# Two weight clamps moved to ScalarE, with conversions, outputs and differences issued at other places

## The chip, the cores and the metric

One core of a Trainium2 chip runs the whole program. Five engines take part: TensorE (PE, with its weight loads PEld), VectorE (DVE), ScalarE (ACT), GpSimd (POOL) and SyncE (SP, which here issues loads and stores). Each engine runs its own list of instructions in order and waits for others by semaphores. The metric is the time of one execution on the device in microseconds (us), as the median of several runs.

## The reference, cut to what matters

```python
# attention: batch 2, seq 3008, d_model 256, d_qk 64
scores = matmul(z, z.transpose(0, 2, 1)) / S
x = u * matmul(maximum(scores, 0.0) ** 2, v)        # 6016 tokens of 256
# first network: w_in 256 x 2048, w_out 2048 x 256
h = x @ w_in;  x = (h - tanh(h)) @ w_out
# second network, with weights of its own
h = x @ w_in
g = where(h >= 1, h, where(h <= -1, 0, (h + 1) ** 2 / 4))
x = g @ w_out
```

The weights come as 64-bit floating point words; the kernel turns them into 32-bit ones itself.

## The kernel before

**Attention.** For each batch, six chunks `c` of 512 queries (the last 448) go over 12 pairs `t` of key tiles, 144 pairs in all, counted here from 0. An *own* pair has its scores `sc` made by TensorE (L361); ScalarE takes the Relu `r` (L386) and the square `hi` (L389), the square at full precision (`a` or `ax`) is made by ScalarE (L397) or in chunk 0 also by VectorE (L404), and VectorE makes the remainder `lo` (L409). The product with `v` (L424) takes `hi` and `lo` one after the other, 16 and 8 matmuls. A *mirrored* pair (those in `MIRROR`) makes no scores: the block was made and stored by an earlier chunk (`mir<-ax`), comes back as `m`, is transposed in two steps by VectorE (`am`, L329), rounded by ScalarE (L343), and VectorE makes `lo` (L347). The product of a pair runs two pairs behind its scores (`LAG`).

**A chunk's end.** Of four accumulators ScalarE copies two to `y` (L469), VectorE adds the other two (L470), and then multiplies by `u` in `scaled` (`ut<-y`, L478). `scaled` is put on the list `deferred`, which `flush` empties in a step of the next chunk.

**Weights.** There are 32 pieces (16 units of weights, each with an input and an output half). For each, the generator `convert` issues seven steps on VectorE and yields a price after each: two masks (L207, L209), two clamps of the exponent `e` (L213, L217), the two parts of the mantissa put together (L215), the sign (L219), the product (L224, to `win` or `wout`). Three later steps stand on the list `posts`: sums on GpSimd, the rounding `phin` or `phout` on ScalarE (L240), the remainder `plin` or `plout` on VectorE (L245). `work(amount)` adds its amount to a credit and issues steps while it is positive. In attention `make(i)` calls it with `CONVERT[0]` for an own pair of chunks 1 to 5 other than a chunk's first; in the first network `fill` calls it with `CONVERT[1]`.

**Networks.** Both run in units of 512 tokens by 128 hidden columns, as seven products of differences and sums of blocks. TensorE puts a product into a bank `m` (L656), ScalarE and VectorE take it out (L592, L595), apply the function (L608, L618), round it (L592) and make its remainder (L629), and TensorE multiplies by the output weights (L675). The differences of the first unit (`t`, L531) and their parts `xht` (ScalarE, L550) and `xlt` (VectorE, L566) are made beside the last pairs of attention; the list `mid` holds those of its steps that run within the unit itself, and the last pair's `lo` among them.

**What sets the order.** All engines' orders follow from the order in which this program issues; no scheduler moves anything later.

## Time and profile before

| what | value |
|---|---|
| median of 3 runs | 1446.07 us (1445.56 to 1447.16) |
| the profiled execution, on the device | 1448.0 us |
| its span from first to last instruction | 1446.2 us |
| TensorE busy | 1426.9 us, 99% |
| VectorE busy | 1250.8 us, 86% |
| ScalarE busy | 983.5 us, 68% |
| GpSimd busy | 106.2 us, 7% |
| mean granted TensorE clock | 0.998 |

TensorE is the busiest engine. What it lacks are single stretches in which it waits. They are found in the list of waits and looked at one by one in the engines' order of time. In a row of that view the first number is the start in us from the span's start, the second the time of the row's instructions together, and in brackets stands how long the engine was idle before and what released it. Instructions of an engine overlap: the next one often starts 0.06 to 0.1 us before the one ahead is shown as ended.

### The profile page before, as it was taken

The page shows a single profiled execution, that of the slowest core. Times are in us where ns is not written, and L with a number is a line of the kernel's source. Part 1 is how long each engine was busy: PE and PEld are TensorE (multiplying, and loading weights), DVE is VectorE, ACT ScalarE, POOL GpSimd, SP SyncE. Part 2 cuts the span into 40 slices and gives each one's busy share as a digit, 9 for nine tenths or more (in the row PEclk, how much of TensorE's full clock was granted, in tenths as well). Part 3 has the DMA queues.
Part 4 walks back from the last instruction along what each step waited for, and adds up shares of the span by engine and source line. Part 5 has one row for each costly group of instructions (what it writes and reads, how often), then busy time and mean ns, then how long its engine had stood idle before and what let it go on. Part 6 is the DMA issues. An engine that isn't in the chain of part 4 may idle for free.

```text
span 1446.2 us, 22024 instructions
## 1 busy us (share of the span) xinstructions
PE 1426.9 (99%) x8293; PEld 1187.9 (82%) x8293; DVE 1250.8 (86%) x1551; ACT 983.5 (68%) x1209; POOL 106.2 (7%) x163
## 2 busy tenths in 40 slices
PE   9999999999999999999999999999999999999998
PEld 6888788988777888888888888987888878788897
DVE  7989899898988888898988888889888888988775
ACT  8887657888654767767676767666666666666543
POOL 0122010031100011010101010000000000000000
PEclk9999999999999999999999999999999999999999
DMA  8899996799898557383765747482564644456361
GB/s 197 256 309 258 245 215 153 233 294 273 240 238 263 182 177 296 114 311 122 259 242 188 273 168 299 137 305 93 170 223 174 204 166 134 161 182 226 119 204 26
DMA packets 274203, 301.11 MB, mean 208 GB/s; under 512 B 134960, under 2 KB 210608, under 8 KB 274096
## 3 DMA queue, kind: packets, MB, share of 16 engines
q1 hardware_dynamic: 261408, 258.53, 57.4%
q0 software_dynamic: 11488, 40.90, 8.0%
q8 instruction: 65, 1.06, 0.3%
q10 hardware_dynamic: 1200, 0.26, 0.1%
q14 instruction: 42, 0.34, 0.1%
HBM read 225.84 MB, written 73.79 MB: 207 GB/s over the span
## 4 chain that ended last, share of the span: by engine, by line
PE 78%; DVE 9%; ACT 5%; DMA 3%; SPq 3%; issue 2%; DVEq 0%; ACTq 0%
PE acc L675 31%; PE m L656 27%; PE acc L424 13%; PE h L849 3%; PE sc L361 2%; DVE lo L409 2%; PE acc L885 2%; DMA m<-mir 1%; DVE am L329 1%; PE acc L906 1%; SPq L316 1%; DVE lo L347 1%; ACT r L386 1%; ACT gha L592 1%; DMA mir<-ax 1%
## 5 line engine op out<-in xcount | busy, mean ns | idle before, releaser
L424 PE MATMUL acc<-hi,v 64*128 64x512 f32 (+1 forms) x2256 | 289.3, 384 | 2.3 <-DVE y L470 2.2
L424 PEld LDWEIGHTS acc<-hi,v 64*128 64x128 f32 x2256 | 225.6, 184 | 39.9 <-DVE y L470 4.7
L656 PE MATMUL m<-xht,w 128*128 128x512 f32 (+1 forms) x704 | 216.1, 388 | 0.0
L675 PE MATMUL acc<-ghb,w 128*128 128x512 f32 (+1 forms) x704 | 187.8, 388 | 0.0
L675 PE MATMUL acc<-gha,w 128*128 128x512 f32 (+1 forms) x704 | 173.3, 387 | 0.0
L424 PE MATMUL acc<-lo,v 64*128 64x512 f32 (+1 forms) x1104 | 158.0, 387 | 7.4 <-DVE lo L409 4.4
L675 PEld LDWEIGHTS acc<-ghb,w 128*128 128x128 f32 x704 | 131.1, 188 | 28.1 <-ACT ghb L592 0.3
L675 PEld LDWEIGHTS acc<-gha,w 128*128 128x128 f32 x704 | 132.2, 188 | 26.3
L656 PEld LDWEIGHTS m<-xht,w 128*128 128x128 f32 x704 | 132.5, 188 | 25.5
L618 DVE TENSOR_TENSOR ta<-ha,ta 128x1024 f32<-128x1024 f32 (+1 forms) x88 | 107.0, 1216 | 40.4 <-ACT ta L615 29.4
L656 PE MATMUL m<-xlt,w 128*128 128x512 f32 (+1 forms) x352 | 137.8, 392 | 2.5 <-DVE xlt L566 1.2
L629 DVE TENSOR_TENSOR gla<-ta,gha 128x1024 fp32r<-128x1024 f32 (+1 forms) x88 | 106.7, 1213 | 33.8 <-ACT gha L592 32.9
L424 PEld LDWEIGHTS acc<-lo,v 64*128 64x128 f32 x1104 | 110.5, 184 | 30.4 <-DVE lo L409 9.7
L592 ACT ACTIVATE u<-m 128x512 f32<-128x512 f32 (+1 forms) x176 | 102.6, 583 | 35.3 <-PE m L656 34.0
L592 ACT ACTIVATE ghb<-tb 128x1024 fp32r<-128x1024 f32 (+1 forms) x88 | 92.6, 1053 | 47.8 <-DVE tb L618 46.9
L629 DVE TENSOR_TENSOR glb<-tb,ghb 128x1024 fp32r<-128x1024 f32 (+1 forms) x88 | 106.5, 1210 | 16.9 <-ACT ghb L592 16.3
L618 DVE TENSOR_TENSOR tb<-hb,tb 128x1024 f32<-128x1024 f32 (+1 forms) x88 | 106.5, 1210 | 5.0 <-ACT tb L608 0.2
L343 ACT ACTIVATE hi<-am 128x1024 fp32r<-128x1024 f32 (+1 forms) x60 | 61.4, 1023 | 70.0 <-DVE am L329 56.5
L656 PE MATMUL m<-xhb,w 128*128 128x512 f32 (+1 forms) x352 | 107.7, 387 | 0.0
L592 ACT ACTIVATE gha<-ta 128x1024 fp32r<-128x1024 f32 (+1 forms) x88 | 92.2, 1048 | 17.8 <-DVE ta L618 17.1
L386 ACT ACTIVATE r<-sc 128x1024 f32<-128x1024 f32 (+1 forms) x83 | 84.1, 1013 | 27.7 <-PE sc L361 26.1
L615 ACT ACTIVATE ta<-ta 128x1024 f32<-128x1024 f32 x40 | 42.4, 1061 | 78.4 <-DVE ta L610 78.4
(115 smaller groups left out, 2538.0 us busy)
## 6 DMA issues: line engine op xcount, KB each, us to landing
w<-packed SPq DMA_DIRECT2D x288, 512.0 KB, 6.4
mir<-ax SPq DMA_DIRECT2D x50, 512.0 KB, 4.5
m<-mir SPq DMA_DIRECT2D x200, 128.0 KB, 4.5
xr<-kept SPq DMA_DIRECT2D x20, 512.0 KB, 7.2
packed<-phin POOLq DMA_DIRECT2D x16, 512.0 KB, 4.1
packed<-plin POOLq DMA_DIRECT2D x16, 512.0 KB, 4.7
widein<-in_moe_w_in_dram POOLq DMA_DIRECT2D x15, 512.0 KB, 6.7
wideout<-in_moe_w_out_dram POOLq DMA_DIRECT2D x15, 512.0 KB, 8.1
```

Of the source, the lines that this page charges most:

```text
L343: nc.scalar.activation(out=hi[s], in_=a[s], func=AF.Copy)
L361: nc.tensor.matmul(ps[:, j, :n], zs[b, g][half, x, k0 : k0 + P], q[half, y, :n], start=(k == 0), stop=(k == 2))
L386: nc.scalar.activation(out=r[s], in_=ps[s], func=AF.Relu)
L409: lows.append(lambda: nc.vector.tensor_tensor(out=lo_, in0=to, in1=hi_, op=ALU.subtract))
L424: nc.tensor.matmul(acc[d][h][:, :n], lhsT, g[half, j, :n], start=start, stop=stop)
L592: nc.scalar.activation(out=out_, in_=in_, func=AF.Copy)
L615: nc.scalar.activation(out=self.t[self.s], in_=self.t[self.s], func=AF.Square, scale=0.5, bias=0.5)
L618: nc.vector.tensor_tensor(out=self.t[self.s], in0=self.h[self.s], in1=self.t[self.s], op=ALU.subtract if self.net == 0 else ALU.max,)
L629: nc.vector.tensor_tensor(out=self.lo[self.s], in0=self.t[self.s], in1=self.hi.bitcast(F32)[self.s], op=ALU.subtract)
L656: nc.tensor.matmul(bank[:, : self.w], self.win[wp][:, block, :], xop[self.net, self.s][x][xp], start=start and i == 0, stop=True, skip_gro ...
L675: nc.tensor.matmul(self.acc(d, n)[:, : self.w], self.wout[:, part, j, d * P : (d + 1) * P], g[:, at, : self.w], start=start, stop=stop,)
L849: nc.tensor.matmul(banks[j][:, :n], win[wp][:, 2 * k + j, :], x[:, k, :n], start=(k == 0 and i == 0), stop=(k == 1 and i == 2),)
```

## The change

It has five parts.

1. In `convert`, the two clamps of the exponent are two Relu of ScalarE where `state["scalar"]` is set: in chunks 2 to 5 and in the first network. 52 instructions of VectorE go and 52 of ScalarE come; 12 clamps stay on VectorE, in chunk 1. The price of both is then not counted in the credit. The product's yields and the moment at which the next piece's load is issued move along.
2. `make` issues no conversion in a chunk's first three pairs; `CONVERT[0]` is 2.0 instead of 1.8, the credit is cut at 2.0, and no new steps start while three or more wait in `posts`. A mirrored pair issues a step from `posts` that costs nothing by the prices (the sums on GpSimd or the rounding on ScalarE). At the end of attention 16 pieces are done instead of 18; the first network converts the rest.
3. `scaled` is issued by the new list `scales`, behind the second score product of the next chunk; in chunks 2 to 5 that is behind the two transposes of a mirrored pair.
4. In a chunk's second pair the full-precision square by VectorE (`product`, chunk 0) is put on the list `tail`, and so comes behind the adds of `y`.
5. In the first unit of the first network, the first four steps of `mid` (two differences, their rounding, the last pair's `lo`) come ahead of the add of `ha`; one `z` block at the start is transposed and cut a pair later.

TensorE's order stays as it was. On GpSimd and SyncE a few loads change places.

```diff
-CONVERT = 1.8, 1.4
+CONVERT = 2.0, 1.4
...
-        return [(dma, AHEAD), (turn, 3), (cut, 2)]
+        late = (b, g) == (0, 2)
+        return [(dma, AHEAD), (turn, 3 - late), (cut, 2 - late)]
...
-        nc.vector.tensor_scalar(out=es, in0=ei, scalar1=-896.0 * 2**20, scalar2=0.0, op0=ALU.add, op1=ALU.max)
-        yield 0.42
+        if state["scalar"]:
+            nc.scalar.activation(out=e, in_=es, func=AF.Relu, scale=-8.0, bias=1151.0 * 2**23)
+            nc.scalar.activation(out=es, in_=e, func=AF.Relu, scale=-1.0, bias=255.0 * 2**23)
+        else:
+            nc.vector.tensor_scalar(out=es, in0=ei, scalar1=-896.0 * 2**20, scalar2=0.0, op0=ALU.add, op1=ALU.max)
+            nc.vector.tensor_scalar(out=es, in0=es, scalar1=255.0 * 2**20, scalar2=8.0, op0=ALU.min, op1=ALU.mult)
+            yield 0.84
         nc.vector.scalar_tensor_tensor(out=m, in0=low, scalar=2.0**-32, in1=mi, op0=ALU.mult, op1=ALU.add)
         yield 0.69
-        nc.vector.tensor_scalar(out=es, in0=es, scalar1=255.0 * 2**20, scalar2=8.0, op0=ALU.min, op1=ALU.mult)
-        yield 0.42
...
-            nc.vector.tensor_tensor(out=to, in0=src, in1=src, op=ALU.mult)
-            tail.append(square_hi) if late else square_hi()
+            def product():
+                nc.vector.tensor_tensor(out=to, in0=src, in1=src, op=ALU.mult)
+
+            for fn in (product, square_hi):
+                tail.append(fn) if late else fn()
...
-        deferred.append(scaled)
+        scales.append(scaled)
...
+            if att:
+                for fn in att[2][:4]:
+                    fn()
             self.A = Half(self.net, w, "a")
...
             if att:
-                for fn in att[2]:
+                for fn in att[2][4:]:
                     fn()
                 att[0]()
...
-            state["credit"] += amount
+            state["credit"] = min(state["credit"] + amount, 2.0)
...
-            while converts and state["credit"] > 0:
+            while converts and state["credit"] > 0 and len(posts) < 3:
...
-            if c and (t // 2, c) not in MIRROR and i < NATT - NPA - 1 and at[b, c, t]:
+            state["scalar"] = c > 1
+            if at[b, c, t] < 3 or c == 0 or i >= NATT - NPA - 1:
+                return
+            if (t // 2, c) not in MIRROR:
                 work(CONVERT[0])
+            elif posts and posts[0][0] == 0:
+                posts.pop(0)[1]()
...
                 first_product(i + 1, False)
+                for fn in scales:
+                    fn()
+                scales.clear()
```

**Pair 98**, the third pair of chunk 2 in the second batch. VectorE's order before, from behind the adds of `y` to the pair's `lo` (`lo_4602`); `lo_4555` is that of pair 97, `am` the transposes for the mirrored pair 99:

```order
L215 SCALAR_TENSOR_TENSOR mout0_6_4499<-wideout0_6_4392,mout0_6_4499 128x512
L217 TENSOR_SCALAR eout0_6_4500<-eout0_6_4500 128x512
L219 SCALAR_TENSOR_TENSOR eout0_6_4500<-wideout0_6_4392,eout0_6_4500 128x512
L409 TENSOR_TENSOR lo_4555<-a_4553,hi_4554 128x1024
L478 SCALAR_TENSOR_TENSOR ut1_1_4407<-y_4558,ut1_1_4407 128x1024
L329 STREAM_TRANSPOSE am_4608<-m1_02_0_4211 128x2x256
L329 STREAM_TRANSPOSE am_4608<-m1_02_1_4216 128x2x256
L245 TENSOR_TENSOR plin0_6_4642<-win0_6_4454,phin0_6_4581 128x1024
L224 SCALAR_TENSOR_TENSOR wout0_6_4646<-mout0_6_4499,eout0_6_4500 128x512
L409 TENSOR_TENSOR lo_4602<-ax_4600,hi_4601 128x1024
```

And now (`lo_4559` is pair 98's):

```order
L418 TENSOR_TENSOR lo_4519<-a_4517,hi_4518 128x1024
L335 STREAM_TRANSPOSE am_4564<-m1_02_0_4174 128x2x256
L335 STREAM_TRANSPOSE am_4564<-m1_02_1_4179 128x2x256
L487 SCALAR_TENSOR_TENSOR ut1_1_4371<-y_4522,ut1_1_4371 128x1024
L418 TENSOR_TENSOR lo_4559<-ax_4557,hi_4558 128x1024
```

All five conversion steps are gone from this stretch, and `ut` stands behind the transposes.

**The batch boundary**, pairs 71 to 74. VectorE's order before, from the `lo` of pair 71 to that of pair 74 (`lo_3466`):

```order
L409 TENSOR_TENSOR lo_3332<-a_3330,hi_3331 128x2x448
L404 TENSOR_TENSOR a_3379<-r_3382 128x1024
L111 TENSOR_TENSOR v1_5_3369<-vraw1_5_3209,v1_5_3369 128x512
L409 TENSOR_TENSOR lo_3381<-a_3379,hi_3380 128x1024
L404 TENSOR_TENSOR a_3424<-r_3427 128x1024
L470 TENSOR_TENSOR y_3430<-y_3430,acc01_2975 128x448
L470 TENSOR_TENSOR y_3430<-y_3430,acc11_2977 128x448
L144 STREAM_TRANSPOSE zt1_3_3454<-zraw1_3_3245 128x512
L409 TENSOR_TENSOR lo_3426<-a_3424,hi_3425 128x1024
L478 SCALAR_TENSOR_TENSOR ut0_5_3285<-y_3430,ut0_5_3285 128x2x448
L404 TENSOR_TENSOR ax_3479<-r_3482 128x8x4x32
L409 TENSOR_TENSOR lo_3466<-ax_3464,hi_3465 128x1024
```

And now, the same stretch (`lo_3445` is pair 74's):

```order
L418 TENSOR_TENSOR lo_3304<-a_3302,hi_3303 128x2x448
L411 TENSOR_TENSOR a_3358<-r_3361 128x1024
L112 TENSOR_TENSOR v1_5_3348<-vraw1_5_3181,v1_5_3348 128x512
L418 TENSOR_TENSOR lo_3360<-a_3358,hi_3359 128x1024
L479 TENSOR_TENSOR y_3408<-y_3408,acc01_2945 128x448
L479 TENSOR_TENSOR y_3408<-y_3408,acc11_2947 128x448
L411 TENSOR_TENSOR a_3403<-r_3406 128x1024
L145 STREAM_TRANSPOSE zt1_3_3433<-zraw1_3_3217 128x512
L418 TENSOR_TENSOR lo_3405<-a_3403,hi_3404 128x1024
L411 TENSOR_TENSOR ax_3457<-r_3460 128x8x4x32
L487 SCALAR_TENSOR_TENSOR ut0_5_3257<-y_3408,ut0_5_3257 128x2x448
L418 TENSOR_TENSOR lo_3445<-ax_3443,hi_3444 128x1024
```

The adds of `y` stand ahead of the second `a<-r`, and `ut` behind `ax<-r`. ScalarE there, from `a` of pair 71, before:

```order
L397 ACTIVATE a_3330<-r_3333 128x2x448
L240 ACTIVATE phin0_4_3361<-win0_4_2660 128x1024
L108 ACTIVATE v1_5_3369<-vraw1_5_3209 128x512
L386 ACTIVATE r_3382<-sc_3372 128x1024
L389 ACTIVATE hi_3380<-r_3382 128x1024
L386 ACTIVATE r_3427<-sc_3417 128x1024
```

And now:

```order
L403 ACTIVATE a_3302<-r_3305 128x2x448
L217 ACTIVATE ein0_4_3338<-ein0_4_3338 128x512
L218 ACTIVATE ein0_4_3338<-ein0_4_3338 128x512
L109 ACTIVATE v1_5_3348<-vraw1_5_3181 128x512
L392 ACTIVATE r_3361<-sc_3351 128x1024
L395 ACTIVATE hi_3359<-r_3361 128x1024
```

Where a rounding of a weight piece stood there are the two Relu of another piece, which read what VectorE's mask of that piece writes.

**The first unit of the first network.** VectorE's order before, from `xlt` of the first difference to the part `xhc`; `lo<-a` is that of the last pair of attention:

```order
L566 TENSOR_TENSOR xlt_0_6498<-t_0_6226,xht_0_6374 128x1024
L595 TENSOR_TENSOR ha<-m_6508,m 128x512
L531 TENSOR_TENSOR t_0_6520<-xr_0_1_5990,t_0_6226 128x512
L531 TENSOR_TENSOR t_0_6520<-xr_0_0_5989,t_0_6520 128x512
L409 TENSOR_TENSOR lo<-a,hi 128x2x448
L566 TENSOR_TENSOR xlt_0_6526<-t_0_6520,xht_0_6523 128x1024
L566 TENSOR_TENSOR xhc_0_6528<-xr_0_1_5990,xhc_0_6528 128x512
```

And now:

```order
L575 TENSOR_TENSOR xlt_0_6461<-t_0_6189,xht_0_6337 128x1024
L540 TENSOR_TENSOR t_0_6477<-xr_0_1_5953,t_0_6189 128x512
L540 TENSOR_TENSOR t_0_6477<-xr_0_0_5952,t_0_6477 128x512
L418 TENSOR_TENSOR lo<-a,hi 128x2x448
L604 TENSOR_TENSOR ha<-m_6471,m 128x512
L575 TENSOR_TENSOR xlt_0_6489<-t_0_6477,xht_0_6480 128x1024
L575 TENSOR_TENSOR xhc_0_6491<-xr_0_1_5953,xhc_0_6491 128x512
```

The two differences and the last pair's `lo` stand ahead of the add of `ha`.

## Rows read from the trace of the kernel before

**Rows 1.** Busy time by stage: window, busy us (instructions) by engine, PEclk, DMA share, GB/s.
```profile
0.00:450.00 450.00, 439.13 (x3797) 367.80 (x3797) 402.62 (x532) 336.86 (x375) 59.98 (x94) 1.00 0.89 243
...
464.20:467.60 3.40, 3.15 (x11) 2.27 (x13) 0.91 (x2) 0.91 (x3) 0.00 (x0) 0.50 0.85 293
...
500.00:850.00 350.00, 350.00 (x1545) 289.57 (x1544) 306.21 (x362) 246.76 (x310) 33.47 (x49) 1.00 0.59 211
```

**Rows 2.** TensorE's waits: engine, line, waited for, us in total, times, longest.
```profile
PE acc L424 <- DVE lo L409: 4.4, 6, 1.2
...
PE acc L424 <- DVE lo L347: 2.8, 6, 0.9
...
PE acc L424 <- DVE y L470: 2.2, 5, 1.2
```

**Rows 3.** Groups by line: a clamp on VectorE, a rounding copy on ScalarE (busy, mean ns).
```profile
L213 DVE TENSOR_SCALAR ein<-ein 128x512 int32<-128x512 uint32 x16 | 6.7, 417 | 0.0
...
L240 ACT ACTIVATE phout<-wout 128x512 fp32r<-128x512 f32 x16 | 9.9, 617 | 0.0
```

**Rows 4.** VectorE in order of time ahead of pair 98's lo: start us, us, instruction.
```profile
325.33 1.19 DVE L245 TENSOR_TENSOR plin<-win,phin 128x1024 fp32r<-128x1024 f32 x1
...
326.43 0.69 DVE L224 SCALAR_TENSOR_TENSOR wout<-mout,eout 128x512 f32<-128x512 f32 x1
...
327.03 1.22 DVE L409 TENSOR_TENSOR lo<-ax,hi 128x1024 fp32r<-128x1024 f32 x1
```

**Rows 5.** TensorE in order of time around stalls; in brackets idle before and releaser.
```profile
141.52 0.74 PE L424 MATMUL acc<-lo,v 64*128 64x512 f32 x4 [0.80 <-DVE lo L409]
...
176.09 0.73 PE L424 MATMUL acc<-lo,v 64*128 64x512 f32 x4 [0.45 <-DVE lo L347]
...
240.04 0.74 PE L424 MATMUL acc<-hi,v 64*128 64x512 f32 x4 [1.21 <-DVE y L470]
...
326.32 0.80 PE L424 MATMUL acc<-hi,v 64*128 64x512 f32 x4
...
328.30 0.50 PE L424 MATMUL acc<-lo,v 64*128 64x512 f32 x2 [1.19 <-DVE lo L409]
```

**Rows 6.** The same view of TensorE, first unit of the first network.
```profile
462.80 0.50 PE L656 MATMUL m<-xlt,w 128*128 128x512 f32 x1 [1.21 <-DVE xlt L566]
...
464.45 0.79 PE L656 MATMUL m<-xlt,w 128*128 128x512 f32 x1 [0.69 <-ACT u L592]
```

**Rows 7.** VectorE in order of time, first unit.
```profile
458.37 0.69 DVE L595 TENSOR_TENSOR ha<-m,m 128x512 f32<-128x512 f32 x1 [1.58 <-PE m L656]
...
458.97 1.41 DVE L531 TENSOR_TENSOR t<-xr,t 128x512 f32<-128x512 f32 x2
...
461.51 1.23 DVE L566 TENSOR_TENSOR xlt<-t,xht 128x1024 fp32r<-128x1024 f32 x1
```

**Rows 8.** ScalarE in order of time: pair 59, batch boundary, a first-network unit.
```profile
197.08 1.04 ACT L397 ACTIVATE ax<-r 128x1024 f32<-128x1024 f32 x1
...
234.01 1.01 ACT L386 ACTIVATE r<-sc 128x1024 f32<-128x1024 f32 x1
...
618.75 0.60 ACT L592 ACTIVATE u<-m 128x512 f32<-128x512 f32 x1 [0.63 <-PE m L656]
```

**Rows 9.** VectorE in order of time from pair 59's step to the add of y.
```profile
198.24 0.70 DVE L144 STREAM_TRANSPOSE zt<-zraw 128x512 f32<-128x512 f32 x1
...
198.87 1.18 DVE L409 TENSOR_TENSOR lo<-ax,hi 128x1024 fp32r<-128x1024 f32 x1
...
202.88 0.69 DVE L470 TENSOR_TENSOR y<-y,acc 128x512 f32<-128x512 f32 x1 [0.62 <-ACT y L469]
```

**Rows 10.** VectorE in order of time, batch boundary.
```profile
232.57 0.42 DVE L217 TENSOR_SCALAR eout<-eout 128x512 int32<-128x512 int32 x1
...
238.24 1.22 DVE L404 TENSOR_TENSOR a<-r 128x1024 f32<-128x1024 f32 x1
```

**Rows 11.** TensorE in order of time, the same first-network unit.
```profile
620.82 0.39 PE L656 MATMUL m<-xlt,w 128*128 128x512 f32 x1
```

More of the change, by code (lines that the diff above doesn't have):

```diff
@@ L94, in attention_then_two_ffn @@
     lows = []
+    scales = []
     def add_load(first, last, steps, slots=1):
@@ L193, in attention_then_two_ffn @@
     done = set()
+    state = {"credit": 0.0, "step": 0, "scalar": True}
     def convert(net, f, which, src):
@@ L768, in emit @@
                 flush()
+                scales.pop()()
                 due()
@@ L1050, in attention_then_two_ffn @@
         held = {}
-        state = {"credit": 0.0, "step": 0}
         NATT = B * QC * NPA
@@ L1062, in work @@
                 state["credit"] -= cost
-            while converts and state["credit"] > 0:
+            while converts and state["credit"] > 0 and len(posts) < 3:
                 if state["step"] == 0:
                     next(converts[0])
-                elif state["step"] == 4 and len(converts) > 1:
+                elif state["step"] == 3 and len(converts) > 1:
                     next(converts[1])
@@ L1168, in attention_then_two_ffn @@
         mid.append(lambda: turn_u(B - 1, QC - 1))
+        state["scalar"] = True
         p = None
```

## The prediction

> **What bounds the kernel now.** I read the busy time by stage first, then TensorE's waits, then what VectorE and ScalarE do at each place where TensorE stands still. By stage [rows 1] TensorE is busy 439.13 of the first 450 us (attention) and all of 350 in the first network, so time can be won only in attention and in the first unit behind it; the second network isn't touched. The reader sees in the waits [rows 2] what TensorE waits for there: VectorE, with `lo` of an own pair (4.4 us, six times), `lo` of a mirrored pair (2.8, six times) and the add of `y` at a chunk's end (2.2, five times). No wait on ScalarE of that size stands there. VectorE is not late everywhere: it is late at a dozen places where weight conversion, transposes and `lo` queue up in its order, and at each of them the step that ends last is a `lo` (or an add) behind work that nobody waits for.
>
> How a stall is priced: ahead of pair 98's `lo`, four matmuls from 326.32 take 0.80 together [rows 5], where a lone one takes 0.39 [rows 11]; so each begins before the one ahead is shown as ended. The next comes at 328.30, after 1.19 of idle. Without the wait it would have begun before that idle time, so the stall costs more than 1.19, at most by those 0.39 of overlap. I price a stall at its idle time plus 0.26, an estimate between 0 and 0.39; eight stalls make 1 us either way.
>
> **The change part by part.**
>
> *Clamps to ScalarE.* 52 VectorE clamps go (26 pieces, two each) at 0.417 us [rows 3]: 22 in attention, 30 in the first network, 21.7 us in all. 52 Relu come on ScalarE; none is in the trace, the nearest row is a 128x512 copy there, 0.617 [rows 3], 0.52 to 0.60 from start to start, so 27 to 32 us. Neither sum is on the path by itself. What counts is that `eout<-wideout,eout` on VectorE now waits for ScalarE's second Relu, with everything behind it in VectorE's queue, and that the first Relu waits for VectorE's first conversion step, with the next `r` behind it in ScalarE's queue.
>
> The profile has VectorE at 402.62 of 450 us in attention [rows 1], and its clamp is shorter than ScalarE's copy. The Trainium skill (Perfetto Trace Analysis, Optimizing Scalar/DVE Operations) says that VectorE is the faster one where it has a perf mode, and that moving work to ScalarE may make sense if VectorE is saturated. The rows agree on the durations; that VectorE is saturated no row shows, and what the time would be if it were is the third rival below.
>
> *Conversions leave a chunk's first three pairs* (mirrored ones too, where they had none). This is the main term. Pair 98: `plin` 1.19 and `wout` 0.69 [rows 4] stand between the two transposes and `lo`; both go, and the step ahead of `lo` is then `ut`, which was ahead before as well. `lo` starts about where `plin` began, 325.33, and its 1.22 end at 326.55, while TensorE is still in the four matmuls from 326.32: the stall is gone, 1.19 + 0.26 = **-1.46**. At 141.52 idle is 0.80, and of the conversion steps ahead of that `lo` `plout` and two of 0.42 [rows 3] go, while a `wout` of 0.69 comes; three more ahead of the `lo` before go too: 0.80 + 0.26 = **-1.06**. Four stalls of 0.44 to 0.53 (at 64, 176, 369 and 403 us, the one at 176.09 shown) each lose two to four conversion steps in VectorE's queue ahead of them, of 0.42 to 1.19 [rows 3, 4], or get them later: 4 x (0.49 + 0.26) = **-3.0** [rows 5]. Short hesitations at 134, 172 and 291 us: **-0.5**. Late next at these places is nothing that I could find: `lo` gets 0.4 us of slack and more, and the conversions put off come in later own pairs, whose score product gives VectorE more time.
>
> *First unit.* TensorE waits 1.21 for `xlt` [rows 6], which VectorE makes last: add of `ha`, two differences (1.41), `lo` of the last pair, then `xlt` at 461.51 [rows 7]. The differences need nothing of this unit, and are now issued ahead of the add, in the time that VectorE waits for TensorE's product (1.58 idle ahead of 458.37). ScalarE can cut their high part beside `lo`; `lo` (some 1.1), the add (0.69) and `xlt` (1.23) then follow from 458.1 on and end near 460.9, against 461.59, where TensorE's wait began (462.80 less 1.21): 1.21 + 0.26 = **-1.47**. The next stall, 0.69 on a copy of ScalarE, stays. Behind the two the granted clock is 0.50 for 3.4 us [rows 1], the lower of TensorE's levels: 1.7 us lost. The idle of 1.19 at 328.30 and of 1.21 at 240.04 [rows 5] has no such stretch behind it (the clock of the first 450 us is 1.00), so I take it to go with the first stall: **-1.7** (0 if the second alone brings it). The Trainium skill (TensorE: Matmul & The Clock Gate, What's actually happening) ties the clock to how busy TensorE has been; the trace agrees, and says no more on this case.
>
> *Pair 59, a chunk's end: a new wait.* ScalarE's `ax` starts at 197.08 [rows 8]; two Relu follow and end near 199.2. VectorE's two steps behind them (0.60 each from start to start) end at 200.5, where `zt` began at 198.24; from there to the add of `y` were 202.88 - 198.24 - 0.62 idle = 4.02 us of work [rows 9]. So the add starts at 204.5, 1.6 later, and TensorE's next chunk begins behind it. `r` behind the Relu is 0.8 late too. VectorE no longer waits for the second copy, so the stalls in the chunk behind shrink by some 0.3: **+1.3** (0 to +1.6).
>
> *Batch boundary.* The add of `y` waits behind `a<-r` at 238.24 (1.22) [rows 10], and TensorE 1.21 for it [rows 5]. The reorder puts the adds ahead. But the Relu there need `ein`, which VectorE issues behind `plout`: it begins near 233.15 and ends at 233.6, the Relu at 234.8, and `r` at 234.01 [rows 8] moves to 235.2. Everything up to the add is 1.2 late, which eats the 1.1 of the reorder. `a<-r` then starts at 240.4 instead of 238.24; the next `r`, `ax`, now ahead of `ut`, and `lo` of pair 74 follow, which ends near 249.0, some 1.2 after TensorE wants it. **+1.2** (-0.9 if the Relu don't wait, +1.5).
>
> *Start.* One of the six waits on `lo` [rows 2], 0.99, goes with the later `z` block, whose low part is then itself late by about a microsecond: **+0.3** (-1.2 to +0.8). *`ut` behind the transposes*: it fills VectorE while ScalarE rounds, 0. *POOL and SP*: some loads change places, nothing waits for them in attention: 0.
>
> *First network.* TensorE is never idle [rows 1]. ScalarE idles 0.63 ahead of copy `u`, which ends at 619.35 [rows 8]; its bank is wanted at 620.82 [rows 11]: 1.47 of slack. Two Relu ahead of `u` take 1.12, less 0.63: 0.5 late, 1.0 with a rounding beside them. Covered at each of the 15 sites, **+0.5** for jitter with the attention sites together (0 to +5). If that cover is gone, each site costs what is above 1.47.
>
> **Sum.** Gains 1.46 + 1.06 + 3.0 + 0.5 + 1.47 + 1.7 = 9.2; losses 1.3 + 1.2 + 0.3 + 0.5 = 3.3: **-5.9 us**. The trace's span is 1446.2 (its own execution 1448.0), the median of the runs 1446.07; on the median: **1440.2**. With each term at its better end the sum is some -12, at its worse +2 or more.
>
> **The rivals.** (1) *The stalls only move.* A Relu wait costs about 0.7 of VectorE at nine further attention sites as it does at pair 59; for it speaks that VectorE has no idle time over long stretches, against it that at the sites I followed `lo` has 0.5 to 1.7 to spare. 9 x 0.7 = 6.3: 1446.5. That the change does less than it says (the clamps freed lie where VectorE would have waited anyway, and only the first unit gains 3.2, less 2.5 of new waits) ends at the same place, 1445.4. (2) *Slower*: ScalarE becomes the bound in the first network. In its queue stand rounding, two Relu and `u`; if the first Relu waits for VectorE by a further 0.5, `u` ends 1.5 to 2.2 later than now and the product behind waits up to 0.7 and 0.26 at each of 15 sites: +14, 1454. It decides from a delay of 1.47 on; for it speaks that VectorE is busy 306 of 350 there, against it that the first conversion step is issued behind `tb`, before `ghb` is done. (3) *VectorE is the bound throughout*: the time falls by what is freed in attention beside the gains above, 22 x 0.34 = 7.5: 1432.7. Against it: the waits [rows 2] are 9.4 us in 450. By the Trainium skill (Perfetto Trace Analysis, Optimizing Scalar/DVE Operations) this is where offloading pays.
>
> **How the numbers follow.** Forecast 0.60 (1436.5 to 1443.5 by the start, the clock, the boundary and pair 59); stalls move 0.20; slower 0.10; VectorE bound throughout 0.10. The likeliest is 1440.2. The range takes the forecast's own, half of each of the neighbours: 1434.0 to 1446.5. A difference under 0.2% (2.9 us) can't be told from none; faster by more (under 1443.2): 0.56 of the forecast, the 0.10 and a little of the first rival, 0.72; same 0.19; slower 0.09.
>
> **What would show it.** Right: no idle ahead of `lo` at pair 98, at 141 or of `xlt`, and no half clock behind it; new idle ahead of the second matmul of the chunk after pair 59 (about 1.5 to 2 us in all) and ahead of `lo` of pair 74; ScalarE up by about 30 us, VectorE down by 22; the first network without idle. Wrong: waits of TensorE on a copy `u` in the first network, `lo` late in chunks 2 and 3 behind `eout<-wideout,eout`, or the half clock still there.

## The result: 13 us slower, and the profile after

The changed kernel takes **1458.8 us** (median; 1457.65 to 1461.49) against 1445.93 (1445.25 to 1447.16) in the same comparison: ratio **1.0091**, 95% interval 1.0078 to 1.0104. The forecast was 1440.2 with a range up to 1446.5, so its sign is wrong. The profiled execution took 1461.49, its span is 1459.7.

Read the stages first (columns as in [rows 1]). In attention TensorE loses 1.3 us of busy time against before; in the first network, where it had not been idle in this window [rows 1], it now stands still for 6.9 of 350.

```profile
0.00:450.00 450.00, 437.80 (x3780) 378.88 (x3782) 382.66 (x492) 346.78 (x393) 55.34 (x85) 0.99 0.86 234
500.00:850.00 350.00, 343.12 (x1499) 279.80 (x1498) 297.80 (x345) 250.60 (x325) 38.43 (x58) 1.00 0.61 216
```

TensorE's waits say for whom (as in [rows 2]). `lo L418`, `y L479` and `lo L353` are attention's; their sum is smaller than before without the one wait of 3.5. The two that stand in the product `m` are new, and both belong to the first network: there TensorE waits for a bank `m` that ScalarE copies, and for `ha`, which VectorE adds.

```profile
PE m L665 <- ACT m L601: 5.1, 6, 1.9
PE acc L433 <- DVE lo L418: 5.1, 3, 3.5
PE m L665 <- DVE ha L604: 4.1, 4, 1.7
PE acc L433 <- DVE y L479: 2.3, 7, 0.8
PE acc L433 <- DVE lo L353: 1.9, 4, 0.8
```

Here is what the forecast had not priced: two queues that wait for one another. This is ScalarE and then VectorE and TensorE around 540 us of the changed kernel (start, us, instruction, idle before and releaser). ScalarE has a copy, a rounding of 1.06 and a rounding of 1.04 to do before it comes to the two Relu; VectorE, whose order has the sign step next, waits 2.65 for them, and `wout`, `glb` and `ha` stand behind. TensorE waits 1.74 for that `ha`. In all, VectorE waits 9.7 us for a second Relu in 500 to 950 us, at six of the 15 sites.

```profile
536.83 1.04 ACT L246 ACTIVATE phin<-win 128x1024 fp32r<-128x1024 f32 x1
537.78 0.61 ACT L217 ACTIVATE eout<-eout 128x512 f32<-128x512 int32 x1
538.42 0.63 ACT L218 ACTIVATE eout<-eout 128x512 int32<-128x512 f32 x1
...
539.09 0.69 DVE L225 SCALAR_TENSOR_TENSOR eout<-wideout,eout 128x512 uint32<-128x512 uint32 x1 [2.65 <-ACT eout L218]
...
540.43 1.22 DVE L638 TENSOR_TENSOR glb<-tb,ghb 128x1024 fp32r<-128x1024 f32 x1
541.56 0.68 DVE L604 TENSOR_TENSOR ha<-u,m 128x512 f32<-128x512 f32 x1
...
542.30 0.96 PE L665 MATMUL m<-xhc,w 128*128 128x512 f32 x3 [1.74 <-DVE ha L604]
```

The other direction, around 888 us: ScalarE waits 1.37 for VectorE's mask `ein`, which stands behind VectorE's `glb` and `ha`. Its `ta` comes behind the two Relu, VectorE waits 1.14 for `ta`, ScalarE's `gha` for VectorE, the copy `m` stands behind `gha` and two copies to `y`, and TensorE waits 1.90 for `m`.

```profile
887.92 0.43 DVE L210 TENSOR_SCALAR ein<-widein 128x512 uint32<-128x512 uint32 x1
...
888.38 0.63 ACT L217 ACTIVATE ein<-ein 128x512 f32<-128x512 int32 x1 [1.37 <-DVE ein L210]
889.05 0.63 ACT L218 ACTIVATE ein<-ein 128x512 int32<-128x512 f32 x1
889.59 0.94 ACT L617 ACTIVATE ta<-ha 128x896 f32<-128x896 f32 x1
...
890.55 1.09 DVE L627 TENSOR_TENSOR ta<-ha,ta 128x896 f32<-128x896 f32 x1 [1.14 <-ACT ta L617]
...
893.49 0.55 ACT L601 ACTIVATE m<-m 128x448 f32<-128x448 f32 x1
...
894.09 0.47 PE L665 MATMUL m<-xlt,w 128*128 128x448 f32 x1 [1.90 <-ACT m L601]
```

The second new loss is at the start. VectorE's transpose of a later `z` block waits 3.66 for its DMA, `lo` stands behind it, and TensorE is idle for 3.52. In the kernel before, the same transpose (last row below) waited 1.43, and TensorE 0.39. Behind the 3.52 the granted clock (the eighth column of the window row) is 0.50, the lower of the two levels, for 6.8 us.

```profile
36.38 0.71 DVE L145 STREAM_TRANSPOSE zt<-zraw 128x512 f32<-128x512 f32 x1 [3.66 <-DMA zraw<-in_z_dram]
37.02 1.18 DVE L418 TENSOR_TENSOR lo<-ax,hi 128x1024 fp32r<-128x1024 f32 x1
...
38.25 2.08 PE L433 MATMUL acc<-lo,v 64*128 64x512 f32 x8 [3.52 <-DVE lo L418]
...
37.15:43.98 6.83, 5.73 (x28) 4.51 (x30) 6.83 (x8) 6.12 (x7) 0.00 (x0) 0.50 1.01 272
```

```profile
31.95 0.71 DVE L144 STREAM_TRANSPOSE zt<-zraw 128x512 f32<-128x512 f32 x1 [1.43 <-DMA zraw<-in_z_dram]
```

**Where the time went, matmul by matmul.** TensorE's order is the same in all kernels of this study and all 8293 matmuls are in each trace, so the same matmul's start in two traces, subtracted, gives the time lost (+) or won since the one before it. Stretches by the time of the kernel before, us; the last three columns are kernels of the experiments below.

| stretch (before) | forecast | changed | no Relu | one by one | ut back |
|---|---|---|---|---|---|
| 1 to 50, start | +0.3 | +7.00 | +0.32 | +0.28 | +0.83 |
| 50 to 195 (64, 134, 141, 172, 176) | -2.9 | -3.95 | -4.61 | -4.13 | -3.59 |
| 195 to 207, pair 59 | +1.3 | +1.51 | -0.18 | -0.22 | -0.20 |
| 207 to 265, batch boundary | +1.2 | +1.15 | +1.51 | +1.23 | +0.57 |
| 265 to 335 (291, pair 98) | -1.6 | -1.95 | -1.39 | -0.58 | -1.43 |
| 335 to 457 (369, 403) | -1.5 | -1.40 | -2.13 | -2.14 | -2.15 |
| 457 to 534, first unit | -3.2 | -1.95 | -1.95 | -1.92 | -1.95 |
| 534 to 895, first network | +0.5 | +13.23 | +4.69 | +1.46 | +1.46 |
| rest | 0 | -0.18 | -1.07 | -0.33 | -0.22 |
| sum | -5.9 | +13.47 | -4.79 | -6.35 | -6.69 |

(The forecast's shares by stretch are its terms, with the four stalls at 0.75 each and the short ones at 0.17 each.) What was forecast to be won was won, 9.2 us of gains forecast against 9.3 in the four stretches; two terms that were forecast near nothing cost 20.

Each column compares one profiled execution with one of the kernel before, and these lie at different places among the times of their kernels: 1448.0 of the kernel before (median 1445.93), 1461.49 of the changed one (1458.8), 1443.21 of the one without Relu (1444.85), for the last two just the median. So the sums, and small differences between columns, are good to 2 to 3 us only; for what a version is worth the times below count. In attention the matmuls start in twos, so that the edge of a stretch can shift 0.2 into its neighbour. In the three last columns the row "rest" holds a gain of some 0.96, from 895 us on, that is no idle time. The matmuls of 448 columns follow one another there every 0.203 us, in the kernel before every 0.207, with a clock of 1.00 in both. Why, no run shows.

### The profile page after: what moved, and what is told of

It is laid out like the page before. It is cut to its first block, busy times and chain, and to the rows that moved or that the text cites. A ratio compares the mean times of both kernels' runs of the same rounds, so it can differ in the third digit from the quotient of the medians.

```text
span 1459.7 us, 22001 instructions
## 1 busy us (share of the span) xinstructions
PE 1430.4 (98%) x8293; PEld 1198.3 (82%) x8293; DVE 1229.7 (84%) x1499; ACT 1010.2 (69%) x1261; POOL 106.8 (7%) x163
## 3 DMA queue, kind: packets, MB, share of 16 engines
q8 instruction: 65, 1.06, 0.3%
## 4 chain that ended last, share of the span: by engine, by line
PE 76%; ACT 9%; DVE 9%; DMA 2%; issue 2%; SPq 1%; DVEq 0%; ACTq 0%
PE acc L684 27%; PE m L665 23%; PE acc L433 18%; PE sc L367 3%; PE h L862 3%; PE acc L898 1%; PE acc L919 1%; DVE tb L627 1%; DVE glb L638 1%; ACT r L392 1%; ACT gha L601 1%; DMA zraw<-in_z_dram 1%; DVE ta L627 1%; SPq L322 1%; DVE ha L604 1%
## 5 line engine op out<-in xcount | busy, mean ns | idle before, releaser
L433 PE MATMUL acc<-hi,v 64*128 64x512 f32 (+1 forms) x2256 | 300.2, 385 | 2.3 <-DVE y L479 2.3
L433 PEld LDWEIGHTS acc<-hi,v 64*128 64x128 f32 x2256 | 239.3, 185 | 34.3 <-DVE y L479 4.7
L433 PE MATMUL acc<-lo,v 64*128 64x512 f32 (+1 forms) x1104 | 168.8, 386 | 7.0 <-DVE lo L418 5.1
L433 PEld LDWEIGHTS acc<-lo,v 64*128 64x128 f32 x1104 | 123.5, 185 | 23.8 <-DVE lo L418 7.1
```

The costliest lines, as they stand in the source:

```text
L433: nc.tensor.matmul(acc[d][h][:, :n], lhsT, g[half, j, :n], start=start, stop=stop)
```

## The experiments

The theory from these rows: in the first network it is the waits between the two queues that cost, and at the start the later `z` block. The rival: ScalarE's own time, in the first network some 19 us more work (30 Relu of 0.63), is what pushes its copies back. Another: two weight pieces more are converted in the first network, 16 in place of 14.

**Clamps of the first network back on VectorE,** at the Relus' very places and without a price for the planner, so that nothing else moves.

```diff
-            yield 0.84
+            if not state.get("free"):
+                yield 0.84
...
-        state["scalar"] = True
+        state["scalar"], state["free"] = False, True
```

> The changed kernel with the two clamps of the 15 pieces of the first network on VectorE again, issued at the very place where the two Relu stood (no price in the credit, so every other instruction keeps its place). Theory A: the 9.3 us of TensorE's idle time in the first network come from VectorE's sign step waiting for ScalarE's second Relu and from ScalarE's Relu waiting for VectorE's mask, with ha, glb and ta queued behind them; the idle time falls under 1 us and the time by 9 to 11, to about 1448 (2 above the kernel before). Rival B: it comes from 16 pieces being converted there instead of 14, so VectorE, with 12.5 us more to do, is later still: idle 9 or more and 1458 to 1465.

1451.98 us, ratio 1.0039 (1.0025 to 1.0053). The first network loses 4.73 in place of 13.23. 8.5 us come with the Relu; 4.7 are lost without any, more than was expected.

**The `z` block at its old place.**

```diff
-        late = (b, g) == (0, 2)
+        late = False
```

> The changed kernel with the third z block transposed and cut where it was before. Theory A: the later transpose frees the buffer of z loads later, SP's queue behind it runs 3 us late, and the z block at 36 us comes 4.4 us late; undone, the 3.5 us wait of TensorE there is 0.4 as before, no half clock stands behind it, and the time falls by 2.5 to 6, to 1453 to 1456. Rival B: the wait was chance of the profiled run (its time was 2.7 above the median): the time stays within 1 us of 1458.8.

1455.63, ratio 1.0063 (1.0049 to 1.0077). The start loses 0.47 in place of 7.00, no half clock is left behind it, and no other stretch changes by more than the one around pair 98 (310 to 335 us: -1.09 against -1.66).

**Both.**

> Both: clamps of the first network on VectorE, z block early; what is left of the change is attention's part and the first unit. Theory A (the prediction's terms for these hold: -9.2 of stalls that go, +1.3 and +1.2 of new ones at pairs 59 and 74): 1438 to 1442, 4 to 8 below the kernel before. Rival B (attention's gains are given back elsewhere): 1445 to 1447.

1446.6, ratio 1.0005 (0.9996 to 1.0014). So the two together explain the whole loss against the kernel before. But the gain of 4 to 8 us that was expected beyond that isn't there, and the rival's time came: of what attention and the first unit win, the first network still eats 4.71, and pair 59 and the boundary some 2.8.

**Both, and attention's clamps on VectorE too:** no Relu is left, all reorders stay.

```diff
-            state["scalar"] = c > 1
+            state["scalar"], state["free"] = False, c > 1
```

> As the one above, with the 22 clamps of attention on VectorE too, at the places of the Relu: no Relu is left, the reorders stay. Theory A (Relu on ScalarE cost attention the new waits at pairs 59 and 74 and save nothing on TensorE's path): 1 to 3 us faster than the one above, 1437 to 1440. Rival B (VectorE is short of time in attention, so 7.5 us more on it bring stalls of lo back): 2 to 6 slower than the one above.

1444.85, ratio 0.9991 (0.9982 to 1.0). By the times it is 1.75 us ahead of the kernel with both, by the matmuls of the profiled executions (of which this one was the fastest of its kernel) 3.4: pair 59's loss is gone (+1.5 to -0.18), and 50 to 195 and 335 to 457 win 0.7 and 0.7 more. So the attention gains don't come from the offload. They come from where the conversions stand, and the Relu eat a part.

**The two suspects put into the kernel before.** First its own order with the first network's clamps as Relu (the two `nc.vector.tensor_scalar` of a clamp replaced from the first unit on), then only the later `z` block.

```diff
-        nc.vector.tensor_scalar(out=es, in0=ei, scalar1=-896.0 * 2**20, scalar2=0.0, op0=ALU.add, op1=ALU.max)
-        yield 0.42
+        if state["scalar"]:
+            nc.scalar.activation(out=e, in_=es, func=AF.Relu, scale=-8.0, bias=1151.0 * 2**23)
+            nc.scalar.activation(out=es, in_=e, func=AF.Relu, scale=-1.0, bias=255.0 * 2**23)
+        else:
...
```

> The kernel before with one part of the change alone: the clamps of the pieces converted in the first network (13) are two Relu of ScalarE. Attention, its conversions (18 pieces done there) and everything else as before. Theory A (the waits between VectorE's and ScalarE's queues cost what the clamps back on VectorE gave back, 9 us of 13): TensorE idles 6 to 10 us in the first network, time 1453 to 1457. Rival B (two pieces more in the first network make the loss, not the Relu): under 2 us of idle, 1446 to 1448.

> The kernel before with the third z block transposed and cut a pair later, nothing else. Theory A (SP's queue of z loads runs late behind the buffer that this transpose frees): TensorE waits 2 to 3.5 us more near 33 us, time 1448.5 to 1452. Rival B (it only shows together with the other parts): within 1 us of the kernel before.

1453.21, ratio 1.004 (1.0024 to 1.0055), 5.12 lost in the first network; and 1452.07, ratio 1.0028 (1.0015 to 1.004), 5.31 lost at the start (a wait of 2.74 on `lo`, then 3.4 us of half clock). Each alone makes the kernel before slower. In its order, where a piece's steps are issued one by one and 13 pieces fall into the first network in place of 15, the Relu cost 5.1, in the changed one 8.5 over the clamps.

**Mask, Relu and sign in three different stops of the planner,** so that no queue should wait for the other, with a larger credit (2.0 in place of 1.4) to get the pieces done, on the kernel with the early `z` block.

> The changed kernel with the z block early and all Relu kept, but in the first network a piece's masks, its Relu and its sign step are issued in three different calls (the credit per call raised from 1.4 to 2.0 so that the pieces are ready in time): neither engine finds its partner's step still to come. Against the changed kernel with the z block early alone (1455.6). Theory A (the waits between the two queues make the loss, not ScalarE's 17 us of extra work): the first network loses 2 to 5 us instead of 13, 1445 to 1448. Rival B (ScalarE's work itself is too much for a unit): 10 or more are lost, 1453 to 1457.

1456.53, ratio 1.0058 (1.0044 to 1.0072); 11.99 lost in the first network. VectorE's waits for `eout` are gone and TensorE's for `ha` with them, and yet the time is no better. It seemed to speak for ScalarE's own time. But some 1.5 of the 11.99 are clock: behind a wait of 1.80 for `m` at 719.32 the granted clock is 0.50 for 3.4 us.

```profile
719.72:723.13 3.41, 3.41 (x10) 2.64 (x9) 2.95 (x5) 2.67 (x4) 0.00 (x0) 0.50 1.03 310
```

And the larger credit did something of its own, as VectorE's order ahead of 646 us, where TensorE loses 1.0, shows: three conversion steps between `ha` and `ta`, 2.5 us from start to start, where ScalarE then waits 2.05 for `ta`.

```profile
639.78 0.69 DVE L609 TENSOR_TENSOR ha<-u,m 128x512 f32<-128x512 f32 x1 [1.39 <-ACT u L606]
640.39 1.22 DVE L256 TENSOR_TENSOR plin<-win,phin 128x1024 fp32r<-128x1024 f32 x1
641.52 0.69 DVE L230 SCALAR_TENSOR_TENSOR eout<-wideout,eout 128x512 uint32<-128x512 uint32 x1
642.25 0.69 DVE L235 SCALAR_TENSOR_TENSOR wout<-mout,eout 128x512 f32<-128x512 f32 x1
642.85 1.22 DVE L632 TENSOR_TENSOR ta<-ha,ta 128x1024 f32<-128x1024 f32 x1
...
644.11 1.06 ACT L606 ACTIVATE gha<-ta 128x1024 fp32r<-128x1024 f32 x1 [2.05 <-DVE ta L632]
```

So this run mixes several things and decides nothing; that the credit makes the rest of its loss is argued from this one place, not shown. The next two separate work and wait.

**ScalarE's work without the wait, and the wait without the work,** both on the kernel with both (clamps on VectorE). In the first, two Relu on a spare tile of 448 columns that nobody else uses; in the second, Relu of 8 columns that read VectorE's mask, which VectorE's clamp then overwrites and so waits for (it waits for the first of the two Relu, where the changed kernel's sign step waits for the second).

```diff
+                nc.scalar.activation(out=spare, in_=spare.bitcast(I32), func=AF.Relu, scale=-8.0, bias=1151.0 * 2**23)
+                nc.scalar.activation(out=spare.bitcast(I32), in_=spare, func=AF.Relu, scale=-1.0, bias=255.0 * 2**23)
```

```diff
+                nc.scalar.activation(out=spare[:, :8], in_=es[:, :8], func=AF.Relu, scale=-8.0, bias=1151.0 * 2**23)
+                nc.scalar.activation(out=spare.bitcast(I32)[:, :8], in_=spare[:, :8], func=AF.Relu, scale=-1.0, bias=255.0 * 2**23)
```

> The version with the clamps of the first network on VectorE and the early z block (ratio 1.0005), with two Relu more on ScalarE at the places where the changed kernel has its own, on a spare tile of 448 columns that nobody else reads or writes: ScalarE's work without any wait between the queues. Theory A (the first network's 13 us are the waits between VectorE and ScalarE): loses about what the version without them lost there, 4.7 to 6: ratio 1.0005 to 1.002, near 1447 to 1449. Theory B (ScalarE's time itself pushes its next copies and tanh back): 11 to 14 lost there, ratio 1.005 to 1.007, near 1455. In between both count.

> The same version with two Relu of 8 columns at the same places: the first reads VectorE's masked exponent, and VectorE's clamp, which overwrites it, waits for that: the waits between the queues in both directions, nearly without ScalarE's work. Theory A (the waits): 8 to 13 us lost in the first network, ratio 1.004 to 1.006. Theory B (ScalarE's time): 4.7 to 6 lost, ratio 1.0005 to 1.002.

Work alone: 1447.82, ratio 1.0007 (0.9998 to 1.0016). Wait alone: 1459.57, ratio 1.0086 (1.0072 to 1.01). In the first network 5.86 and **15.80** are lost, against 4.71 without either; VectorE keeps its clamps in all three. The groups by line show what each adds (busy us, mean ns): 17.2 us of ScalarE's work cost 1.15, some 6 us of it in Relu of 8 columns that are waited for cost 11.1.

```profile
L225 ACT ACTIVATE spare<-spare 128x448 int32<-128x448 f32 x15 | 8.7, 580 | 0.5
L224 ACT ACTIVATE spare<-spare 128x448 f32<-128x448 int32 x15 | 8.5, 565 | 0.0
```

```profile
L225 ACT ACTIVATE spare<-spare 128x8 int32<-128x8 f32 x15 | 3.1, 209 | 0.5
L224 ACT ACTIVATE spare<-eout 128x8 f32<-128x8 int32 x8 | 1.6, 196 | 3.1 <-DVE eout L213 3.1
L224 ACT ACTIVATE spare<-ein 128x8 f32<-128x8 int32 x7 | 1.4, 199 | 2.7 <-DVE ein L213 2.7
```

TensorE's waits in 500 to 950 us, first without either, then with the work alone, then with the wait alone. Only the last has waits on `ha`: 7.8, six times, the kind of stall shown above at 540.

```profile
PE m L666 <- ACT m L602: 3.5, 5, 1.1
```

```profile
PE m L672 <- ACT m L608: 3.9, 5, 1.3
```

```profile
PE m L672 <- DVE ha L611: 7.8, 6, 2.2
PE m L672 <- ACT m L608: 4.5, 5, 1.4
```

The theory of the waits holds, and the rival of ScalarE's time falls.

**The clamps priced one by one.** What are the 4.7 us that are left without Relu? In that kernel a clamp had no price, so up to three VectorE steps stood in one stop. Here each has its 0.42 and a stop of its own, with a credit of 1.6.

```diff
-CONVERT = 2.0, 1.4
+CONVERT = 2.0, 1.6
...
+            if not state.get("free"):
+                yield 0.42
             nc.vector.tensor_scalar(out=es, in0=es, scalar1=255.0 * 2**20, scalar2=8.0, op0=ALU.min, op1=ALU.mult)
-            yield 0.84
+            if not state.get("free"):
+                yield 0.42
...
-        state["scalar"] = True
+        state["scalar"], state["free"] = False, False
```

> The version with no Relu at all (its clamps of the first network stood on VectorE without a price in the planner, so that three VectorE steps could be issued in one stop) with the first network's clamps priced again at 0.42 each, one step at a time as in the kernel before, and a credit of 1.6 a stop so that 16 pieces are ready in time. Theory A (the 4.7 us that are left in the first network come of steps bunched in one stop): the first network loses 0 to 1 us, the gains of attention (8.4 by the end of the first unit) arrive at the end: ratio 0.9945, near 1438. Theory B (two pieces more are converted there, and VectorE has no room for them): 3 to 5 us are still lost, ratio 0.998.

**1441.65** against 1446.58, ratio 0.9964 (0.9951 to 0.9978): faster than the kernel before and than the version that it was made from (0.9991), if less than the 0.9945 that was expected. The first network loses 1.46; the same VectorE instructions, spread, cost 3.2 less than bunched. The 16 pieces are still converted there, so the two more can't account for over 1.46. TensorE's waits on `m` there (500 to 950 us) went from the 3.5 shown above to 1.2:

```profile
PE m L668 <- ACT m L604: 1.2, 3, 0.6
```

**The batch boundary.** +1.37 stays there without any Relu, so the forecast's reason for it (the Relu waits for `ein`) can't be the cause. First, on the kernel without Relu, VectorE's full-precision square goes ahead of the add of `y` again.

```diff
-            for fn in (product, square_hi):
-                tail.append(fn) if late else fn()
+            product()
+            tail.append(square_hi) if late else square_hi()
```

> The kernel without any Relu (1444.9, z block early) with one reorder undone: in a chunk's second pair of chunk 0 VectorE's square comes ahead of the adds of y again. At the batch boundary that kernel loses 1.4 us against the kernel before, as the one with Relu does. Theory A (the square behind the adds makes r, the next square and lo of pair 74 late): the 1.22 us stall there is gone, another of up to 1.4 ahead of it is back; the boundary costs -0.5 to 0.5 against the kernel before, the time is 0.9 to 1.9 lower, 1443 to 1444. Rival B (the multiplication by u behind ax makes it): no change at pair 74, the add later by 1.1: 1445 to 1446.

1444.93, ratio 0.998 (0.9971 to 0.9989). 242 to 265 us loses nothing, but 207 to 242 loses 1.3: TensorE waits for the add of `y` as before. The reorder moves the stall from one place to another. Then VectorE's order at that second place, in the kernel without Relu: `ut` stands ahead of the `lo` for which TensorE waits 1.06.

```profile
241.62 1.23 DVE L412 TENSOR_TENSOR ax<-r 128x1024 f32<-128x1024 f32 x1 [2.55 <-ACT r L393]
242.76 1.08 DVE L488 SCALAR_TENSOR_TENSOR ut<-y,ut 128x896 f32<-128x896 f32 x1
243.76 1.22 DVE L419 TENSOR_TENSOR lo<-ax,hi 128x1024 fp32r<-128x1024 f32 x1
...
245.03 1.20 PE L434 MATMUL acc<-lo,v 64*128 64x512 f32 x8 [1.06 <-DVE lo L419]
```

So the last run puts `ut` behind that `lo`, at the boundary alone, on the version priced one by one.

```diff
             if lows:
                 lows.pop(0)()
+            if scales and pairs[i][2][:2] == (1, 0) and at[pairs[i][2]] == LAG + 1:
+                scales.pop()()
...
-                for fn in scales:
-                    fn()
-                scales.clear()
+                if pairs[i][2][:2] != (1, 0):
+                    for fn in scales:
+                        fn()
+                    scales.clear()
```

> The version without Relu whose clamps are priced one by one (1441.65 against 1446.58, ratio 0.9964), with one VectorE step put back: at the batch boundary the scaled output ut (1.08) is issued behind the lo that TensorE waits 1.06 for there, no longer ahead of it. If ut ahead of lo is what makes that lo late (and not a<-r, which the reordered add of y delays), the stall goes: the stretch from 242 to 265 us of the kernel before loses 0 to 0.3 instead of 1.37, and the ratio is 0.9955, near 1440.3. If a<-r alone makes it late, the stretch still loses 1 or more, ratio 0.9964. Either way a profile tells, since 1 us is below what the times can tell.

1441.34 against 1446.68, ratio 0.9962 (0.9949 to 0.9976). The stretch from 242 to 265 us loses 0.39 in place of 1.37, and no wait on a `lo` is left there; 0.33 more are lost from 207 to 242. The times can't tell it from the run before it; the trace does.

## Why the prediction was wrong

**The step that failed: "Covered at each of the 15 sites" in the first network** (+0.5 forecast, +13.23 measured). It counted ScalarE's time ahead of one copy `u` and compared it with that copy's slack of 1.47. That part held: work alone costs 1.15. Left out were the two waits that the clamp now makes between in-order queues. The forecast had told of exactly these at pair 59 and priced them there within 0.2; in the first network it named them only in the second rival, as a condition "by a further 0.5", and gave them 0.10. At 888 us the first Relu waits 1.37 for VectorE, not 0.5, and at 540 us VectorE waits 2.65 for the second, because at that stop ScalarE had two roundings in its queue; the slack that had to be compared was that of `ha` and of `m`, not of `u`. That rival's time, 1454, is the nearest of all; its reason (ScalarE becomes the bound) is not what happens, since ScalarE is busy 250.60 of 350.

**Start** (+0.3 forecast, +7.00 in the profile, 4 to 5 us by the ratios of the runs with and without it). The failed step is the sentence on POOL and SP: "some loads change places, nothing waits for them in attention: 0". At 31.95 the kernel before already waited 1.43 for such a load. SP issues the loads of that block from 28.31 to 34.09, in the kernel before from 25.41 to 29.73. SP's waits up to 36 us say what held its queue, first in the changed kernel and then in the kernel before: two waits for VectorE's `v`, 5.7 us together, in place of one of 1.6 for `zt` (waits of 1.1 and less not shown).

```profile
SPq L134 <- DVE v L112: 5.7, 2, 3.6
```

```profile
SPq L133 <- DVE zt L144: 1.6, 1, 1.6
```

The `z` and `v` blocks take their raw tiles from one pool of six, so I take it that SP waits for a tile that VectorE frees later. That the loads move with the block was shown, the pool's part in it was not tried.

Half of the 7.00 is clock: 6.83 us at 0.50 are 3.4 us, an estimate.

**The stalls of attention: right.** Pair 98 and 141 have no idle left; forecast -6.0 for all, measured -7.3 in the changed kernel with the Relu in it. The matmul that had waited 1.19 [rows 5] starts in the changed kernel without idle ahead of it:

```profile
332.02 1.24 PE L433 MATMUL acc<-lo,v 64*128 64x512 f32 x8
```

The stretch of pair 98 itself differs between kernels with the same code there (310 to 335 us: -0.16 to -1.66), with short waits of 0.2 to 0.4 near 316 us that come and go. Why was not settled.

**First unit: the stall right, the clock luck** (-3.2 forecast, -1.95 measured). `xlt` is in time. Up to 468 us 2.69 are won (1.27 where `xlt` was waited for, 1.42 by the clock), of which 0.7 are given back by 534. The half clock of [rows 1] is gone, as in every trace with this reorder; but that it hung on the first stall isn't shown. In the experiment that put the Relu into the kernel before, where the order of this stretch stands as it was, the same two waits are there (1.19 and 0.69), and the clock behind them is 1.00:

```profile
462.51 0.50 PE L664 MATMUL m<-xlt,w 128*128 128x512 f32 x1 [1.19 <-DVE xlt L574]
...
464.20:467.60 3.40, 3.40 (x23) 2.53 (x24) 0.69 (x1) 1.70 (x3) 0.00 (x0) 1.00 0.95 307
```

In that trace the stretch is 0.67 shorter than in the profiled execution of the kernel before, without any reorder, so some 1.3 of the 1.95 are the reorder's. The forecast took its -1.7 from a half clock of one execution and subtracted it from the median: of 60 executions of the kernel before in the comparisons, 10 have that one's mean granted clock of 0.998, the others 0.999 or 1.0. The stall was 1.21 idle and gave back 1.27, so the 0.26 that I added to each stall was 0.06 here; the wait of 0.69 on `u` stayed, as forecast:

```profile
463.89 0.50 PE L665 MATMUL m<-xlt,w 128*128 128x512 f32 x1
...
465.54 0.50 PE L665 MATMUL m<-xlt,w 128*128 128x512 f32 x1 [0.69 <-ACT u L601]
```

**Pair 59: right** (+1.3, measured +1.51; -0.18 without Relu). VectorE waits there 3.20 for the second Relu, TensorE then 0.77 for `lo` and, not shown, 0.77 for `y`:

```profile
202.38 0.69 DVE L225 SCALAR_TENSOR_TENSOR eout<-wideout,eout 128x512 uint32<-128x512 uint32 x1 [3.20 <-ACT eout L218]
...
205.58 0.50 PE L450 MATMUL acc<-lo,v 64*128 64x512 f32 x2 [0.77 <-DVE lo L418]
```

**Batch boundary: right in size, wrong in cause** (+1.2, measured +1.15). Not the Relu: the add of `y` ahead of `a<-r` delays that, and `ut`, which had no price of its own here, stands ahead of the `lo` that comes late. The stall needs both: with the add behind `a<-r` again it is gone (and the older one is back), with `ut` behind `lo` 0.98 of 1.37 are.

**VectorE bound throughout** (third rival): no. VectorE fell from 402.62 to 382.66 in the first 450 us, and with the clamps back on it attention was faster. The moved clamps cost 8.5 us in the first network and some 2 (times) to 3.4 (traces) in attention. The Trainium skill (Perfetto Trace Analysis, Optimizing Scalar/DVE Operations) says only that offloading work to ScalarE "may make sense" if VectorE is saturated. No run here has VectorE saturated over a stage; what the runs show is the case in which it waits at places.

## What to carry to other kernels

Moving a step out of the middle of a chain to another engine added two waits between in-order queues here, and each brought with it what stood ahead in the other queue; price it by what stands in both queues at that stop, at every site, and not by the moved step's time. Work that nobody is waiting for does harm when it comes in threes: the same clamps one to a stop cost 3.2 us less than bunched. A step that seems to fill idle time and a load that "changes places" need a row each: who is next behind them, and when must that be done.

## What the runs showed of the hardware

Relu of 128x512 on ScalarE took 0.61 to 0.63 us, from int32 to float and from float to int32, as much as the float copy of [rows 3] (0.617); with 8 columns it took 0.20. TensorE's granted clock was at the lower of its two levels behind an idle time of 3.52 (for 6.8 us) and, in the kernel before with the later `z` block, of 2.74 (for 3.4 us). From the length of shorter waits it couldn't be told. Behind the waits of 1.74 and 1.90 in the first network of the changed kernel it did not fall, as the windows below show (clock in the eighth column), nor behind one of 2.21 in the run with the wait alone; behind one of 1.80 in the run with three stops it did. Behind 1.21 and 0.69 within 3 us it fell in the kernel before [rows 1, 6], and behind 1.19 and 0.69 in the same place it did not in the kernel before with Relu in the first network. So a half clock of 3.4 us in one profiled execution is not yet a property of the kernel.

```profile
542.30:546.00 3.70, 3.70 (x16) 3.09 (x17) 3.17 (x4) 2.89 (x4) 1.27 (x2) 1.00 1.01 406
894.00:898.00 4.00, 3.91 (x19) 3.58 (x20) 4.00 (x6) 2.93 (x5) 0.54 (x1) 1.00 1.04 333
```
